# The first attention round of batch 0: transposes on TensorE, v in one piece, division after the product

## The chip, the cores and the metric

The kernel runs on one core of one Trainium2 chip. Its engines are named as in the profile: PE is TensorE, DVE is VectorE, ACT is ScalarE, POOL is GpSimd, SP is SyncE, which here only issues DMAs. The metric is the device time of one execution in microseconds (us). The time before is the median of three runs.

## The reference

Attention with pooled queries feeds a bilinear network. There are 4 batches of 8 heads, 1152 tokens and 64 columns a head; the network has 512 inputs and 1536 hidden columns.

```python
q_pool = q.reshape(B, H, S // 2, 2, D).mean(axis=3)
scores = (1 / sqrt(D)) * q_pool @ k.T                 # 576 x 1152 per head
attn = exp(scores - scores.max(-1)); attn = attn / (attn.sum(-1) + 1e-9)
x = (attn @ v), heads put side by side                # 2304 x 512
out = ((x @ w_a) * (x @ w_b)) @ w_out                 # 2304 x 512
```

All inputs and the output are fp32. q and k are drawn with a spread of about 0.55, the weights of the network come as 64-bit words (their float64 form), which the kernel turns into two parts each.

## The kernel before

**Blocks, passes, rounds.** Two heads make a pair, four pairs a batch. A block is 128 pooled queries (or 64 of both heads) of one head against its 1152 keys. Per block: `qk` puts the scores into PSUM (`sps`, two places of 1152 columns), `sm_max` (DVE, L692) copies them to `s` with their row maximum, `sm_exp` (ACT, L699) takes the exponential in place with its row sum, `sm_sum` and `sm_rec` (DVE) make the reciprocal of the sum, `sm_hi` (ACT, L712) writes the probabilities in fp16 to `p`, `sm_lo` (DVE, L716) the rest that fp16 lost, and one DMA transpose (SP, L722) brings both parts, keys in the partitions, to `pt`. After the two blocks of a row pair, `pv` (L752) multiplies them with v, which `v_hi` (ACT, L515) and `v_lo` (DVE, L518) have split into two fp16 parts as well: three products for each of 9 chunks of keys and both heads, 54 matmuls into `xps`. `x_copy`, `x_hi`, `x_lo` and `x_scale` bring the result to the input of the network, again in two parts.

Batch 0 takes two rounds: the first handles rows 0 to 255 of all four pairs ("even", passes 0 to 3, 16 blocks), the second the other rows. So tile 0 of the network (256 rows) can begin as soon as the first round is through. The scores of batch 0 and 1 are fp32 products.

**Weights.** For each of 12 groups f of 128 hidden columns there are three tiles m of 128x512: w_a, w_b and w_out. Each is loaded, and `w_abs` (ACT), `w_max` (DVE, L551, m < 2), `w_tail` (ACT), `w_sign` (POOL, L562) and `w_join` (DVE, L569) make one fp32 tile of the 64-bit words. `w_mag` (DVE, L577), `w_sum` (PE), `w_scale` and `w_inv` (DVE) make a common scale for m < 2; `w_hi` (ACT) and `w_lo` (DVE, L611; POOL, L616, for m = 2) split it.

**The network (MoE).** A tile t of 256 rows takes for each f 24 matmuls (`moe_mm`, L830), an eviction on ACT (`moe_a`, L837), one on DVE (`moe_g`, L842), then a split and `moe_o` (L856).

**Order.** Every step is declared with its engine, a planner's cost, and the names it reads and writes; the order on each engine is written out by hand in `ORDERS`, one list of step numbers per engine. At run time each engine takes its queue strictly in order.

```python
add("ACT", 1.15, i - 3.5, sm_hi, (i,), r=[s, t + "r"], w=[p + "h"])
add("DVE", 1.37 if ps_.split else 1.4, i - 3, sm_lo, (i,), r=[s, p + "h", t + "r"], w=[p + "l"], port=True)
add("SP", 2.97, i, transpose, (i,), r=[p + "h", p + "l"], w=[f"pt{slot}"], gen=0.42, block=1.02)
```

## Time and profile before

| what | value |
|---|---|
| median of 3 runs (lowest, highest) | 851.35 us (850.94, 855.6) |
| the profiled execution: its own time, its span | 852.03 us, 849.8 us |
| busy: PE, DVE, ACT, POOL | 771.8, 644.9, 580.9, 255.1 us |
| mean granted TensorE clock | 0.944 of full speed |
| DMA transposes (SP) | 144 |

The span runs from the first to the last instruction; the profiled execution's own time is 2.2 us longer. Busy time is the union of an engine's instructions; the mean of a group is that of one instruction and includes what overlaps the next.

### The profile page before, as it was taken

To read this page: it belongs to the slowest core of one execution; us is meant where nothing else is said; L and a number is where in the kernel's file an instruction comes from. 1 tells how busy PE (TensorE), PEld (TensorE's weight loads), DVE (VectorE), ACT (ScalarE), POOL (GpSimd) and SP (SyncE) were. 2 spreads that over 40 slices of the span, in tenths; PEclk is the share of its full clock that TensorE was granted. 3 is DMA by queue.
4 is the path that set the end of the run, shared out by engine and by line. 5 is a ranking of instruction groups with operands and counts; after the bars stand their busy time and mean duration, and the time that the engine had idled before them with its cause. 6 is when DMAs were issued, how large, how long until landed. Compare 5 with 4: busy or idle time off the path is not lost.

```text
span 849.8 us, 21268 instructions
## 1 busy us (share of the span) xinstructions
PE 771.8 (91%) x8832; PEld 591.2 (70%) x8832; DVE 644.9 (76%) x1240; ACT 580.9 (68%) x929; POOL 255.1 (30%) x230
## 2 busy tenths in 40 slices
...
GB/s 286 233 246 263 225 222 231 270 180 228 204 208 196 192 217 188 196 191 207 161 215 195 189 193 171 168 200 142 182 159 111 116 93 57 57 27 1 25 1 25
DMA packets 353664, 141.76 MB, mean 167 GB/s; under 512 B 338208, under 2 KB 340256, under 8 KB 353568
## 3 DMA queue, kind: packets, MB, share of 16 engines
...
q14 instruction: 27, 0.22, 0.1%
...
## 4 chain that ended last, share of the span: by engine, by line
PE 53%; DVE 2%; DMA 1%; issue 1%; ACT 0%
PE ab L830 24%; PE ab L856 14%; PE sps L660 8%; PE xps L752 7%; DMA pt<-p 1%; DVE p L716 1%; DVE s L692 1%; DVE g L842 0%; ACT g L837 0%; PE xps L485 0%; DVE vs L518 0%; DVE vmx L481 0%; DVE o L862 0%; PE xps L418 0%; DVE st L709 0%
## 5 line engine op out<-in xcount | busy, mean ns | idle before, releaser
L830 PEld LDWEIGHTS <-wab 128*128 128x128 f16 x2592 | 252.4, 98 | 35.2 <-issue 2.3
L830 PE MATMUL ab<-xt,wab 128*128 128x256 f16 x2304 | 262.3, 274 | 3.2 <-DVE g L842 3.2
L716 DVE SCALAR_TENSOR_TENSOR p<-s,st,p 128x1152 f16<-128x1152 f32 x144 | 206.7, 1439 | 20.1 <-ACT p L712 19.4
L712 ACT ACTIVATE p<-s,st 128x1152 f16<-128x1152 f32 x144 | 178.4, 1248 | 44.8 <-DVE st L709 13.5
L699 ACT ACTIVATE s<-s,st 128x1152 f32<-128x1152 f32 x144 | 179.6, 1248 | 34.6 <-DVE s L692 34.4
L850 POOL TENSOR_TENSOR gl<-g,gh 128x256 fp32r<-128x256 f32 x108 | 94.0, 877 | 328.9 <-ACT gh L847 295.0
L657 PE MATMUL sps<-k,q 64*128 64x512 f32 (+3 forms) x448 | 117.5, 620 | 56.5 <-DVE s L692 36.6
L856 PE MATMUL ab<-wo,gh 128*128 128x512 f32 x432 | 140.0, 405 | 1.7 <-DVE g L842 1.7
L657 PEld LDWEIGHTS sps<-k,q 64*128 64x128 f32 (+1 forms) x448 | 54.0, 210 | 118.8 <-issue 62.9
L752 PE MATMUL xps<-pt,vs 128*64 128x128 f16 (+1 forms) x4320 | 127.4, 219 | 6.6 <-DMA pt<-p 3.8
L752 PEld LDWEIGHTS <-vs 128*64 128x64 f16 x4320 | 117.8, 113 | 19.3 <-issue 16.0
L837 ACT ACTIVATE g<-ab,cc 128x256 f32<-128x256 f32 (+1 forms) x144 | 55.6, 416 | 97.4 <-PE ab L830 97.2
L692 DVE TENSOR_SCALAR_CACHE_REDUCE s<-sps,ksc 128x1152 f32<-128x1152 f32 x72 | 101.0, 1411 | 12.0 <-PE sps L660 11.2
L842 DVE SCALAR_TENSOR_TENSOR g<-ab,cc,g 128x256 f32<-128x256 f32 (+1 forms) x144 | 56.0, 412 | 70.4 <-ACT g L837 70.3
L692 DVE TENSOR_SCALAR_CACHE_REDUCE s<-sps 128x1152 f32<-128x1152 f32 x72 | 96.8, 1349 | 7.7 <-PE sps L657 7.1
L856 PEld LDWEIGHTS ab<-wo,gh 128*128 128x128 f32 x432 | 77.8, 188 | 20.1 <-ACT g L837 1.5
L856 PE MATMUL ab<-wo,gl 128*128 128x512 f32 x216 | 85.5, 396 | 0.0
L847 ACT ACTIVATE gh<-g 128x256 fp32r<-128x256 f32 x108 | 43.4, 411 | 48.5 <-PE ab L856 47.7
L660 PE MATMUL sps<-k,q 64*128 64x512 f16 (+3 forms) x624 | 65.4, 341 | 0.0
L660 PEld LDWEIGHTS <-q 64*128 64x128 f16 (+1 forms) x720 | 36.6, 97 | 39.9 <-issue 7.4
L562 POOL TENSOR_SCALAR xt<-xt 128x512 f16<-128x512 f32 x22 | 53.9, 2449 | 22.0 <-ACT xt L558 17.0
L856 PEld LDWEIGHTS ab<-wo,gl 128*128 128x128 f32 x216 | 40.6, 188 | 10.1 <-POOL gl L850 0.4
...
## 6 DMA issues: line engine op xcount, KB each, us to landing
...
pt<-p SPq DMA_TRANSPOSE x144, 5.5
```

Source lines behind the costliest of these rows:

```text
L657: nc.tensor.matmul(out, q, k, start=True, stop=True)
L660: nc.tensor.matmul(out, q[:, hq], k[:, hk], start=(hq, hk) == (0, 0), stop=(hq, hk) == (1, 0))
L692: nc.vector.tensor_scalar(out=s_t[sbuf(i)], in0=sps[:, at:at + S], scalar1=-1.0 / 16.0 if u is None else ksc[:, u, 4:5], scalar2=None, op0 ...
L699: nc.scalar.activation(out=s, in_=s, func=AF.Exp, scale=-1.0, bias=t[:, 0:1], accum_out=t[:, 1:2])
L712: nc.scalar.activation(out=p_t[pbuf(i)][:, 0], in_=s_t[sbuf(i)], func=AF.Copy, scale=st_t[i % NST][:, 3:4])
L716: nc.vector.scalar_tensor_tensor(out=p[:, 1], in0=s, scalar=st_t[i % NST][:, 3:4], in1=p[:, 0], op0=ALU.mult, op1=ALU.subtract)
L752: nc.tensor.matmul(xps[half(e), at:at + w], vs[:, c, e, hv], pt[:, hp, c, c0:c0 + w], start=(c == 0 and n == 0), stop=(c == NCH - 1 and n ...
L830: nc.tensor.matmul(dst if t < 8 else dst.rearrange("p (b n) -> p b n", b=B), wab[:, f, 1 - m, a, c], moe_x(t, b, c), start=(n == 0), stop= ...
L837: nc.scalar.activation(out=g_t[:, f, c], in_=ab[j][:, 1, c], func=AF.Copy, scale=cc[:, b, f, 0:1])
L842: nc.vector.scalar_tensor_tensor(out=g, in0=ab[j][:, 0, c], scalar=cc[:, b, f, 1:2], in1=g, op0=ALU.mult, op1=ALU.mult)
L850: nc.gpsimd.tensor_tensor(out=gl_t[j], in0=g_t[:, f], in1=gh_t[j].bitcast(F32), op=ALU.subtract)
L856: nc.tensor.matmul(acc[u], g[:, us], wo[:, f, a], start=(first and n == 0), stop=(last and n == 2))
```

## The change

In the four passes of the first round (`ps_.pe`, `N_PE = 4`), the probabilities are neither divided, split nor sent through a DMA. PE transposes the fp32 exponentials themselves against an identity matrix that POOL makes once (`unity`, in the MoE's g tile): 9 chunks of 128 columns per block, in groups of four or two into the two MoE accumulators (`acc`, that is `ab`), and ACT and DVE in turn (`EVICT`) copy each group to an fp32 view of `pt` (`tr_pe`, `tr_out`). `pv_f` multiplies with unsplit fp32 v, which is loaded alternately to the buffer of the split v and to `vraw`: 18 matmuls per row pair in place of 54. The division comes last: `r_diag` (ACT) writes the reciprocals onto a diagonal, `r_wide` (PE) spreads them over partitions beside the result in `xps`, `r_mul` (DVE) multiplies. v is still scaled by its pair's maximum, now in `x_copy`.

Of the weight steps, the magnitude is taken of the joined tile, by ACT for odd f (an absolute value with a sum) and by DVE for even f; the shift (`w_mag` before) is gone; and `w_lo` of m = 2 goes from POOL to DVE for even f. All five lists in `ORDERS` are new, and their numbers count the new steps, so only the first line of one is shown.

```diff
--- before.py
+++ after.py
@@ -27,6 +27,7 @@
 P_SCALE = 2.0 ** 14
 
 REMN = 64
+N_PE, EVICT = 4, "ADADA"
 N_WHOLE, TWO_ROUNDS = 2, (0,)
 
 XE, XR, XO = 0, 256, 320
...
@@ -54,155 +55,159 @@
 
 ORDERS = (
     (
-        13, 6, 21, 30, 38, 140, 148, 29, 157, 48, 165, 50, 67, 267, 94, 275, 121, 156, 284, 175, 292, 177, 394, 194,
...
+        12, 18, 7, 24, 26, 38, 28, 30, 32, 44, 34, 35, 54, 56, 151, 58, 52, 60, 62, 157, 64, 65, 163, 82, 177, 167,
...
@@ -386,6 +390,13 @@
     kz = [z_t[2][:, 128 * j:128 * j + 128] for j in range(2)]
     kzf = [x.bitcast(F16).rearrange("p (a n) -> p a n", a=2) for x in kz]
 
+    ident, diag = g_t[:, 0, 0:128], [g_t[:, 1 + e, 0:128] for e in range(2)]
+    ptf = pt.rearrange("p a c n -> p (a c n)").bitcast(F32).rearrange("p (a c n) -> p a c n", a=2, c=NCH)
+    vf = [vs.rearrange("p c e h d -> p (c e h d)").bitcast(F32).rearrange("p (c n) -> p c n", c=NCH), vraw]
+
+    def vbuf(p):
+        return (["vsh", "vsl"], ["vraw"])[p % 2] if p < N_PE else ["vraw"]
+
     pl = Plan()
     add = pl.add
...
@@ -520,9 +531,11 @@
         )
 
     def prep_vmax(p, new, key):
-        add("SP", 2.05, key - 3, load_v, (p,), w=["vraw"], lag=LOAD_LAG)
+        j = p % 2 if new and p < N_PE else 1
+        names = ["vraw"] if j else ["vsh", "vsl"]
+        add("SP", 2.05, key - 3, load_v, (p, j), w=names, lag=LOAD_LAG)
         if new:
-            add("DVE", 1.26, key, v_max, (p,), r=["vraw"], w=[f"vmx{p}"])
+            add("DVE", 1.26, key, v_max, (p, j), r=names, w=[f"vmx{p}"])
             add("PE", 0.22, key - 2, v_sum, (p,), r=[f"vmx{p}", "ones"], w=["xps"])
...
@@ -546,11 +559,17 @@
             out=z_t[zi(n)], in_=raw_t[ri(n)][:, :, 1].bitcast(F32), func=AF.Abs, scale=2.0 ** -112
         )
 
-    def w_max(f, m, n):
-        z = z_t[zi(n)]
-        nc.vector.tensor_scalar(
-            out=z, in0=z, scalar1=2.0 ** -126, scalar2=None, op0=ALU.max, op1=ALU.max, accum_out=wmx[:, f, m:m + 1]
-        )
+    def on_act(f):
+        return f % 2 == 1
+
+    def w_mag(f, m, n):
+        if on_act(f):
+            nc.scalar.activation(out=w_dst(f, m, 0), in_=w_src(m, n), func=AF.Abs, accum_out=wmx[:, f, m:m + 1])
+        else:
+            z = z_t[zi(n)]
+            nc.vector.tensor_reduce(
+                out=wmx[:, f, m:m + 1], in_=z, axis=AX.X, op=ALU.max, apply_absolute_value=True
+            )
 
...
@@ -612,6 +626,10 @@
                 out=w_dst(f, m, 1), in0=w_src(m, n), scalar=wsc[:, 0, f, m:m + 1], in1=w_dst(f, m, 0),
                 op0=ALU.mult, op1=ALU.subtract,
             )
+        elif f % 2 == 0:
+            nc.vector.tensor_tensor(
+                out=w_dst(f, m, 1), in0=w_src(m, n), in1=w_dst(f, m, 0).bitcast(F32), op=ALU.subtract
+            )
         else:
             nc.gpsimd.tensor_tensor(
...
             add("ACT", 0.555, key, w_tail, (n,), w=[rw + "l"], r=[rw])
             add("POOL", 2.5, key, w_sign, (n,), w=[rw + "l"], r=[rw], port=False)
             add("DVE", 0.68, key, w_join, (n,), r=[rw, rw + "l"], w=[z], port=True)
+            if m < 2:
+                last = [f"z{NZ + m}"] if f == NF - 1 else []
+                last += ["raw2"] if f == NF - 2 else []
+                if on_act(f):
+                    add("ACT", 0.66, key, w_mag, (f, m, n), r=[z], w=[f"wmx{f}{m}", f"w{f}{m}h"] + last)
+                else:
+                    add("DVE", 0.6, key, w_mag, (f, m, n), r=[z], w=[f"wmx{f}{m}"])
             if m == 1:
-                add("DVE", 0.07, key, w_mag, (f,), r=[f"wmx{f}0", f"wmx{f}1"], w=[f"wal{f}"])
-                add("PE", 0.2, key - 5, w_sum, (f,), r=[f"wal{f}", "ones"], w=["xps"])
...
+            elif f % 2 == 0:
+                add("DVE", 0.7, key, w_lo, (f, m, n), r=[z, f"w{f}{m}h"], w=[f"w{f}{m}l"], port=True)
             else:
                 add("POOL", 1.3, key, w_lo, (f, m, n), r=[z, f"w{f}{m}h"], w=[f"w{f}{m}l"])
 
@@ -724,6 +748,60 @@
             in_=p_t[pbuf(i)].rearrange("p a n -> p (a n)"),
         )
 
+    def unity():
+        nc.gpsimd.memset(ident, 0.0)
+        nc.gpsimd.affine_select(
+            out=ident, in_=ident, compare_op=ALU.not_equal, fill=1.0, base=0, pattern=[[-1, 128]], channel_multiplier=1
+        )
+
+    def tr_pe(chunks, j):
+        for n, (i, c) in enumerate(chunks):
+            nc.tensor.transpose(acc[j][:, 128 * n:128 * n + 128], s_t[sbuf(i)][:, 128 * c:128 * c + 128], ident)
+
+    def tr_out(chunks, j, on):
+        i, c = chunks[0]
+        m = 64 * (blocks[i].slot - blocks[i].head)
+        src = acc[j][:, 0:128 * len(chunks)].rearrange("p (c n) -> p c n", n=128)
+        dst = ptf[:, blocks[i].head, c:c + len(chunks), m:m + 128] if chunks[1][0] == i else ptf[:, :, c, m:m + 128]
+        if on == "A":
+            nc.scalar.activation(out=dst, in_=src, func=AF.Copy)
+        else:
+            nc.vector.tensor_copy(out=dst, in_=src)
+
+    def r_diag(i, e):
+        nc.scalar.activation(out=diag[e], in_=ident, func=AF.Copy, scale=st_t[i % NST][:, 3:4])
+
+    def r_wide():
+        for e in range(2):
+            nc.tensor.matmul(xps[half(e), 256:384], one.broadcast_to([128, 64]), diag[e], start=True, stop=True)
+
+    def r_mul(j, x0):
+        x = x32[j][:, x0:x0 + 128]
+        nc.vector.scalar_tensor_tensor(
+            out=x, in0=x, scalar=1.0 / P_SCALE, in1=xps[:, 256:384], op0=ALU.mult, op1=ALU.mult
+        )
+
+    def moved(ps_, i0, u):
+        parts = [[(i, c + d) for d in range(4)] for i in (i0, i0 + 1) for c in (0, 4)] + [[(i0, 8), (i0 + 1, 8)]]
+        out = []
+        for n, chunks in enumerate(parts):
+            j, w, on = (n + u) % 2, len(chunks), EVICT[n]
+            of = sorted(set(i for i, _ in chunks))
+            name = f"pt{blocks[i0].slot}x{n}"
+            out.append(name)
+            add("PE", 0.05 + 0.17 * w, i0 - 6, tr_pe, (chunks, j), r=[f"s{sbuf(i)}" for i in of] + ["g0"], w=[f"acc{j}"])
+            add("ACT" if on == "A" else "DVE", 0.07 + 0.11 * w if on == "A" else 0.07 + 0.14 * w, i0 - 3.5, tr_out, (chunks, j, on),
+                r=[f"acc{j}"], w=[name])
+        return out
+
+    def pv_f(p, at, m):
+        for c in range(NCH):
+            for e in range(2):
+                nc.tensor.matmul(
+                    xps[half(e), at:at + 128], vf[p % 2][:, c, 64 * e:64 * e + 64], ptf[:, e, c, m:m + 128],
+                    start=(c == 0), stop=(c == NCH - 1),
+                )
+
...
@@ -741,6 +819,10 @@
         add("ACT", 1.245, i - 3, sm_exp, (i,), r=[t + "m"], w=[s, t + "s"])
         add("DVE", 0.065, i - 5, sm_sum, (i,), r=[t + "s"], w=[t + "t"])
         add("DVE", 0.075, i - 5, sm_rec, (i,), r=[t + "t"], w=[t + "r"])
+        if ps_.pe:
+            e = blocks[i].head
+            add("ACT", 0.19, i - 3, r_diag, (i, e), r=[t + "r", "g0"], w=[f"g{1 + e}"])
+            return
         add("ACT", 1.15, i - 3.5, sm_hi, (i,), r=[s, t + "r"], w=[p + "h"])
         add("DVE", 1.37 if ps_.split else 1.4, i - 3, sm_lo, (i,), r=[s, p + "h", t + "r"], w=[p + "l"], port=True)
         add("SP", 2.97, i, transpose, (i,), r=[p + "h", p + "l"], w=[f"pt{slot}"], gen=0.42, block=1.02)
...
-    def x_copy(j, at, x0, w):
-        nc.scalar.activation(out=x32[j][:, x0:x0 + w], in_=xps[:, at:at + w], func=AF.Copy, scale=1.0 / P_SCALE)
+    def x_copy(j, at, x0, w, p):
+        scale = 1.0 / P_SCALE if p is None else vsc[:, p, 0:1]
+        nc.scalar.activation(out=x32[j][:, x0:x0 + w], in_=xps[:, at:at + w], func=AF.Copy, scale=scale)
 
     def unit(slots, at, w, key):
...
     def leave(ps_, at, x0, w, key):
         j = ps_.jx
-        add("ACT", 0.072 + 0.192 * w / 256, key - 4, x_copy, (j, at, x0, w), r=["xps"],
-            w=[f"x32{j}{c}" for c in range(x0 // 64, (x0 + w) // 64)])
+        add("ACT", 0.072 + 0.192 * w / 256, key - 4, x_copy, (j, at, x0, w, ps_.p if ps_.pe else None),
+            r=["xps"] + [f"vsc{ps_.p}"] * ps_.pe, w=[f"x32{j}{c}" for c in range(x0 // 64, (x0 + w) // 64)])
+        if ps_.pe:
+            add("DVE", 0.22, key - 4, r_mul, (j, x0), r=["xps"], w=[f"x32{j}{c}" for c in range(x0 // 64, (x0 + w) // 64)])
 
...
@@ -924,6 +1009,7 @@
             self.p, self.again, self.parts = p, again, parts
             self.ends = ()
             self.whole = b > 0
+            self.pe = n < N_PE
             self.split = b >= N_WHOLE
             self.u = n % 2
             self.jq, self.jx = 1 if self.split else n % 2, 0
@@ -976,17 +1062,18 @@
...
     def attend(m):
         ps_ = passes[m]
         b = ps_.p // NP
-        if not ps_.again:
+        if not ps_.pe and (not ps_.again or passes[m - 1].pe):
             prep_v(ps_.p, ps_.base - 1)
         split_qk(ps_, ps_.base - 8)
...
@@ -1000,7 +1087,14 @@
                 i += 1
             if r == 1 and nxt and not nxt.again:
                 prep_vmax(nxt.p, nxt.parts[0] == "even", ps_.end - 4)
-            unit(slots, at, w, i - 1)
+            if ps_.pe:
+                parts = moved(ps_, i - 2, r)
+                add("PE", 2.2, i - 10, pv_f, (ps_.p, at, 64 * slots[0]), r=[f"pt{t}" for t in slots] + parts + vbuf(ps_.p),
+                    w=["xps"], mode=2)
+                add("PE", 0.3, i - 10, r_wide, (), r=["g1", "g2", "ones"], w=["xps"], mode=2)
+                leaving = [(at, XE + at, 128)]
+            else:
+                unit(slots, at, w, i - 1)
             for span in leaving:
                 leave(ps_, *span, i - 1)
             if splits:
```

Three places show how the queues change. First PE, from the first row of the program after the opening scores. The rows of before (`sps` is the scores' PSUM, `xps` that of the product with v; the last two go on in the same way for the 54 matmuls of a row pair, and for those of the next):

```order
L657 MATMUL sps<-k_69,q_73 128x512 x4
L657 MATMUL sps<-k_69,q_73 128x128
L485 MATMUL xps<-vmx,one 128x2
L657 MATMUL sps<-k_69,q_73 128x128
L657 MATMUL sps<-k_69,q_73 128x512 x4
L657 MATMUL sps<-k_69,q_73 128x128 x2
L657 MATMUL sps<-k_68,q_74 128x512 x4
L657 MATMUL sps<-k_68,q_74 128x128 x2
L752 LDWEIGHTS vs
L752 MATMUL xps<-pt,vs 64x128
```

and of the changed kernel, from the first small sum on (`ab_100` and `ab_101` are the two accumulators, `s_75` and `s_76` the exponentials of the two heads, `g` the identity or the diagonal):

```order
L496 MATMUL xps<-vmx,one 128x2
L759 MATMUL ab_100<-g,s_75 128x128 x4
L759 MATMUL ab_101<-g,s_75 128x128 x4
L681 MATMUL sps<-k_69,q_73 128x512 x4
L681 MATMUL sps<-k_69,q_73 128x128
L759 MATMUL ab_100<-g,s_76 128x128 x4
L759 MATMUL ab_101<-g,s_76 128x128 x4
L759 MATMUL ab_100<-g,s_75 128x128
L759 MATMUL ab_100<-g,s_76 128x128
L681 MATMUL sps<-k_69,q_73 128x128
L800 MATMUL xps<-pt,vs 64x128 x18
L776 MATMUL xps<-g,one 64x128 x2
```

The next scores (L681) moved in between the transposes, and the product with v and the wide reciprocal (L800, L776) stand ahead of the third pair's scores.

Second ACT, from its first exponential on, before (`p` are the fp16 probabilities, `o`, `z`, `wab`, `xt` and `g` hold weights here):

```order
L699 ACTIVATE s_75,st<-s_75,st 128x1152
L515 ACTIVATE vs<-vraw,vsc 128x18x64
L712 ACTIVATE p_81<-s_75,st 128x1152
L699 ACTIVATE s_76,st<-s_76,st 128x1152
L558 ACTIVATE g<-g 128x512
L712 ACTIVATE p_82<-s_76,st 128x1152
L545 ACTIVATE z_91<-wab 128x512
L558 ACTIVATE wab<-wab 128x512
L545 ACTIVATE wab<-g 128x512
L699 ACTIVATE s_77,st<-s_77,st 128x1152
L699 ACTIVATE s_75,st<-s_75,st 128x1152
```

and in the changed kernel:

```order
L723 ACTIVATE s_75,st<-s_75,st 128x1152
L558 ACTIVATE z_91<-wab 128x512
L577 ACTIVATE g<-g 128x512
L723 ACTIVATE s_76,st<-s_76,st 128x1152
L767 ACTIVATE pt<-ab_100 128x4x128
L577 ACTIVATE xt_64<-xt_64 128x512
L558 ACTIVATE wab<-g 128x512
L772 ACTIVATE g<-g,st 128x128
L558 ACTIVATE o_90<-xt_64 128x512
L767 ACTIVATE pt<-ab_100 128x4x128
L621 ACTIVATE wo<-z_91 128x512
L767 ACTIVATE pt<-ab_100 128x2x128
```

The scaling to fp16 and v's split are gone; evictions (L767) and diagonals (L772) stand there, with more weight steps between two exponentials.

Third SP, whose queue holds all loads, near its start, before (`p` goes to `pt` by a DMA transpose):

```order
L539 DMA xt_64<-in_w_ab_dram 128x1024
L539 DMA wab<-in_w_out_dram 128x1024
L403 DMA qraw<-in_q_dram 128x2x256
L397 DMA vraw<-in_v_dram 128x1152
L722 DMA_TRANSPOSE pt<-p_81 128x18x128
L539 DMA xt_64<-in_w_out_dram 128x1024
L722 DMA_TRANSPOSE pt<-p_82 128x18x128
L539 DMA wab<-in_w_ab_dram 128x1024
L403 DMA qraw<-in_q_dram 128x2x256
L539 DMA g<-in_w_ab_dram 128x1024
L722 DMA_TRANSPOSE pt<-p_83 128x18x128
L722 DMA_TRANSPOSE pt<-p_81 128x18x128
```

and in the changed kernel:

```order
L414 DMA qraw<-in_q_dram 128x2x256
L552 DMA xt_64<-in_w_ab_dram 128x1024
L411 DMA k_68<-in_k_dram 128x1152
L552 DMA xt_64<-in_w_ab_dram 128x1024
L408 DMA vraw<-in_v_dram 128x1152
L552 DMA g<-in_w_ab_dram 128x1024
L552 DMA wab<-in_w_ab_dram 128x1024
L411 DMA k_69<-in_k_dram 128x1152
L414 DMA qraw<-in_q_dram 128x2x256
L552 DMA xt_64<-in_w_out_dram 128x1024 x2
L408 DMA vs<-in_v_dram 128x1152
L414 DMA qraw<-in_q_dram 128x2x256
```

The transposes of the first round are out of it, and the loads that stood behind them moved up; the first DMA transpose is now the 42nd entry of the queue, before it was the 13th.

## Rows read from the trace of the kernel before

**Rows 1.** The page, part 1: busy time, share of the span, instructions.
```profile
PE 771.8 (91%) x8832; PEld 591.2 (70%) x8832; DVE 644.9 (76%) x1240; ACT 580.9 (68%) x929; POOL 255.1 (30%) x230
```

**Rows 2.** Stretch, length, busy PE, PEld, DVE, ACT, POOL; granted clock, DMA share, GB/s.
```profile
10.00:151.40 141.40, 83.42 (x660) 51.68 (x657) 133.37 (x274) 117.09 (x173) 95.95 (x50) 0.67 0.99 242
10.00:153.50 143.50, 85.43 (x674) 53.19 (x671) 135.47 (x278) 118.35 (x176) 97.33 (x50) 0.68 0.98 241
147.10:250.00 102.90, 97.32 (x1249) 72.26 (x1248) 89.08 (x166) 80.19 (x123) 40.37 (x34) 0.98 1.09 218
250.00:800.00 550.00, 546.86 (x6629) 430.87 (x6629) 418.10 (x794) 373.84 (x613) 110.92 (x131) 1.00 0.80 150
50.00:60.00 10.00, 8.07 (x70) 5.35 (x69) 9.93 (x16) 9.87 (x19) 8.36 (x5) 0.56 0.98 264
150.00:160.00 10.00, 9.37 (x77) 6.92 (x74) 9.51 (x20) 8.46 (x15) 5.70 (x4) 1.00 0.93 319
```

**Rows 3.** Who waited for whom, 10 to 147 us: total, times, longest.
```profile
PE sps L657 <- DVE s L692: 34.6, 17, 3.7
```

**Rows 4.** DVE, 0 to 153 us, groups: busy us, mean ns, idle before them.
```profile
L716 DVE SCALAR_TENSOR_TENSOR p<-s,st,p 128x1152 f16<-128x1152 f32 x23 | 33.1, 1444 | 0.8 <-ACT p L712 0.7
...
L551 DVE TENSOR_SCALAR_CACHE_REDUCE o<-o 128x512 f32<-128x512 f32 x10 | 6.8, 676 | 3.9 <-ACT o L545 3.9
...
L577 DVE TENSOR_SCALAR wal<-wmx 128x2 int32<-128x2 int32 x11 | 4.7, 428 | 0.1
```

**Rows 5.** ACT, 0 to 151.4 us, groups of the same kind.
```profile
L699 ACT ACTIVATE s<-s,st 128x1152 f32<-128x1152 f32 x24 | 29.9, 1246 | 7.2 <-DVE s L692 7.2
L712 ACT ACTIVATE p<-s,st 128x1152 f16<-128x1152 f32 x23 | 28.3, 1244 | 5.8 <-DVE st L709 4.4 <-issue 1.4
L558 ACT ACTIVATE xt<-xt 128x512 int32<-128x512 uint32 x18 | 11.8, 657 | 4.6 <-DMA xt<-in_w_ab_dram 4.6
...
L782 ACT ACTIVATE xt<-x 128x256 f16<-128x256 f32 x4 | 1.6, 403 | 0.0
L761 ACT ACTIVATE x<-xps 128x256 f32<-128x256 f32 x4 | 1.4, 361 | 0.0
```

**Rows 6.** Groups by form over the whole run: evictions from PSUM.
```profile
L842 DVE SCALAR_TENSOR_TENSOR g<-ab,cc,g 128x256 f32<-128x256 f32 x96 | 45.6, 478 | 48.4 <-ACT g L837 48.2
...
L862 DVE COPY o<-ab 128x512 f32<-128x512 f32 x9 | 6.2, 687 | 34.2 <-PE ab L856 34.2
...
L864 ACT ACTIVATE o<-ab 128x512 f32<-128x512 f32 x9 | 5.3, 589 | 5.6 <-PE ab L856 5.6
```

**Rows 7.** PE in order of time: start us, length us, line, idle before.
```profile
7.11 3.69 PE L657 MATMUL sps<-k,q 64*128 64x512 f32 x10 [7.11 <-DMA k<-in_k_dram]
...
99.67 2.20 PE L657 MATMUL sps<-k,q 64*128 64x512 f32 x10
107.27 0.79 PE L657 MATMUL sps<-k,q 64*128 64x128 f32 x2 [5.40 <-DVE st L703]
...
112.18 4.07 PE L657 MATMUL sps<-k,q 64*128 64x512 f32 x10 [3.60 <-DVE s L692]
118.91 0.49 PE L657 MATMUL sps<-k,q 64*128 64x128 f32 x2 [2.66 <-DVE s L692]
...
147.12 1.48 PE L830 MATMUL ab<-xt,wab 128*128 128x256 f16 x12
```

**Rows 8.** The padded score product (L657), weight loads, 210 to 260 us.
```profile
L657 PEld LDWEIGHTS sps<-z,q x12: 186/188/189, 214.8 to 258.9; 128*128 128x128 f32 x12
```

**Rows 9.** Who writes pt, 0 to 147 us: ns min/median/max.
```profile
L722 SPq DMA_TRANSPOSE pt<-p x21: 2689/3979/5616, 18.0 to 144.3; - x21
```

**Rows 10.** ACT in order of time around its first MoE eviction.
```profile
149.70 0.66 ACT L558 ACTIVATE xt<-xt 128x512 int32<-128x512 uint32 x1
150.27 0.70 ACT L607 ACTIVATE wab<-wab,wsc 128x512 f16<-128x512 f32 x1
151.41 0.47 ACT L837 ACTIVATE g<-ab,cc 128x256 f32<-128x256 f32 x1 [0.43 <-PE ab L830]
```

23 lines of the change are left out of this document (9 added, 14 removed), and 284 rows, old and new, of the table ORDERS.

## Prediction

> **What bounds the kernel now.** I read the page first: PE is busy 91% of the span [rows 1]. Where the other 9% lie shows in busy time by stretch, which I cut where tile 0 of the MoE begins (first matmul 147.12 us, [rows 7]; first ACT eviction 151.41, [rows 10]). From 250 to 800 us PE is busy 546.9 of 550, from 147 to 250 it is 97.3 of 102.9: from 147 on PE is the bound and only work taken from PE can shorten that part [rows 2]. Before it, from 10 to 151.4, PE is busy 59% at a mean granted clock of 0.67, ACT 117.1 of 141.4 (83%), and DVE, to its own first MoE step at 153.5, 135.5 of 143.5 (94.4%) [rows 2]. Who waits for whom says the same: PE's largest wait is for L692, DVE's row maximum, 34.6 us [rows 3]. So the span is "DVE's work until tile 0 can start" plus about 700 us of PE work. A microsecond saved ahead of 147 on the engine that sets that point is a microsecond of the total.
>
> **The change, engine by engine, up to tile 0.** The PE queue of after has 78 score products ahead of the first MoE matmul (before: 83), the same v work and all MoE work behind it. So I count what stands in each queue ahead of its first MoE instruction, before and after, and price the difference with mean durations.
>
> DVE loses 16 low halves of p (23 to 7; 1.444 each, 23.1 us), 4 low halves of v of the same shape (5.8), 22 weight maxima (0.676, 14.9), 11 shifts (0.428, 4.7) and one row maximum with its small steps (1.6): 50.1 [rows 4]. It gains 16 evictions of four transposed chunks, priced as L862, a DVE copy of 128x512 out of PSUM (0.687, 11.0); 11 reductions of 512 columns and 6 further weight steps of that width (5 of them from POOL), 0.676 each by L551, 11.5; 8 multiplications by the reciprocal, at most L842's 0.478, 3.8 [rows 4, 6]. Net -23.8: 135.5 becomes 111.7.
>
> ACT loses 16 high halves of p and 4 of v (1.244 each, 24.9) and one exponential (1.246 + 0.19). It gains 16 evictions of four chunks (0.589 by L864), 8 of two chunks (0.361 by L761), 16 diagonals of 128 columns (0.30, taken below L782's 0.403 for 256), 10 magnitudes (0.657 by L558, plus an accumulator read of 0.19), 4 more copies out of xps (1.0 in all) and 3 weight steps that now stand ahead (2.0): 28.5 against 26.3 [rows 5, 6]. But successive ACT instructions overlap by 0.09 (one starts at 149.70, lasts 0.66, the next starts at 150.27, [rows 10]); 21 leave and 57 come (accumulator reads counted with their instruction), so 1.9 and 5.1 come off. Net about -1 to -2; I take -2: 115 us after 10 us. ACT's load stays, and **ACT becomes the longest queue**.
>
> PE gains most. Per row pair of the round, 18 transposes and 18 fp32 products with v replace 54 fp16 products. Prices at the two levels come from the score products: five of them 2.20 at the high clock and 4.07 at the low, the lone sixth 0.49 and 0.79 [rows 7]. 13 pairs of blocks: 35 us fast, 63 slow. A transpose is not in this trace. From below it costs one fp32 weight load of 128 columns, 0.188 [rows 8]; from above the lone product, 0.49. I take half a lone product, 0.24 (they run in fours, so the drain is shared): 144 make 35 fast (27 to 71), 58 slow. pv_f, 72 pairs that use both column halves as the score pairs use both row halves: 0.24 and 0.40 each, 18 and 29; if the halves didn't overlap, twice that. The wide reciprocal and the 14 small sums: 11 and 17. Sum 98 us fast, 167 slow, against 83 us busy now.
>
> SP loses 16 DMA transposes, each holding its queue for 3.98 us (median of 21 ahead of 147, [rows 9]), and the DMA engines, at a share of 0.99, lose their traffic [rows 2]. I cost this at nothing by itself, as it only lets loads come earlier. POOL loses 5 low halves, gains the identity matrix, and is busy 96 of 141 [rows 2]. The magnitude of a weight now stands behind POOL's sign step and DVE's join; the cover is the weight tiles of other f in flight. If it were gone, each of the 11 f would hold its w_hi back by about a join and a magnitude, 1.3 us, 15 in all.
>
> **The sum.** ACT needs 115 us after 10 us. At 100% its first MoE eviction comes at 125, at DVE's present share of 94.4% at 132, at ACT's own present 83% at 149. I take 90%, nearer to DVE's share, since ACT is now the queue that others wait for, but below it: DVE (112 in the same 128 us, 87%) and PE (77% if fast) are close behind, and in-order queues of like length lose more to each other than one long queue does. 115/0.90 = 128, so 138 instead of 151.4: 13.6 us earlier. Behind that point nothing is removed from PE; the five products that move behind it (2.2 us) I set against the 5.6 us that PE still idles from 147 to 250. Span 849.8 - 13.6 = 836.2; the profiled execution lies 2.2 above its span (852.03), so 838.4; the median shown, 851.35, is 0.7 below that: **838**.
>
> **The rivals.**
> *ACT and DVE use the room better* (low end). Shares of 94 to 100%: 832 down to 825. For it: loads come earlier, and DVE stops being everybody's wait. Against: an engine next to two nearly full ones.
>
> *A wait takes the place of the one removed.* The transposes go through two PSUM tiles (ab), so each group of four waits for the eviction two groups earlier, which stands in ACT's or DVE's queue behind weight steps; pv_f, the reciprocal and all small sums share one bank (xps), held until ACT's copy and DVE's multiplication are through. ACT's exponentials wait 7.2 us in 24 for DVE, 0.30 each [rows 5]; if the 40 new ACT instructions that wait for PE or DVE lose as much, that is 12 us: 849.8 - 13.6 + 12 gives about 850, no change.
>
> *PE becomes the bound, slower than before.* If PE stays at its low clock in round one, its 167 us, begun 7 us in as now [rows 7], end at 174, not 147: 27 us later, 878. It decides once less than 39% of this work runs at the high level (167 - 0.39 x 69 = 140, the time PE has today). For it: the granted clock is 0.67 now, and a stretch in which PE was busy 8.1 of 10 us had 0.56 [rows 2]. Against it: 9.4 of 10 had 1.00 [rows 2], and the products at 99.67, which came right behind other work, ran at the high level, while those at 107.27, after 5.4 us idle, ran low [rows 7]; more work in the same gaps means fewer such pauses. The Trainium skill (TensorE: Matmul & The Clock Gate, Part 4: PE-mode transpose) says that transposes don't count as busy for the clock, which stays low through them, and gives about 275 ns for one of bf16 in a kernel. By its price the fast sum would be 103 instead of 98 (an estimate from that page), and by its rule this rival is the likelier one; no row here shows a transpose on PE, so neither is borne out yet.
>
> **Chances.** 0.5% (4.3 us) is about what a measurement of this kernel can tell from no change. Forecast, 829 to 847: 0.58. Better than that: 0.10. The new wait, 847 to 855.6: 0.16. PE cold, up to 878: 0.16. The range that leaves no more than two in ten out reaches from ACT without a gap (825) into the first part of the cold case (857). Faster 0.68, same 0.16, slower 0.16; the forecast's own range is 829 to 847.
>
> **What would show it.** Right: the first MoE matmul near 134 and ACT's first MoE eviction near 138; ACT busy about 90% from 10 us to there, DVE below 90%; a granted clock above 0.67 in that stretch; transposes of 0.19 to 0.25; PE still above 99% from 250 to 800. Wrong: transposes at twice that with the clock at its low level; long waits of PE before L759 or L800 for evictions; ACT evictions that wait for PE; w_hi waiting for its scale; or a later part in which PE, now started earlier, waits for DMA transposes or DVE that it did not wait for before.

## The result, and the profile of the changed kernel

The changed kernel takes 841.27 us (median of four runs, 840.6 to 843.49), the kernel before 853.48 beside it (four runs, 850.94 to 855.6): a ratio of 0.986, 95% interval 0.982 to 0.990. It is faster by 1.4%. Forecast were 838 and a range of 825 to 857. The profiled execution took 841.28 us, with a span of 839.5. The same kernel run again as a control (experiment 5) gave 840.71 against 851.51, a ratio of 0.988 (0.986 to 0.990), so of the 13.4 us that were forecast 12.2 came in the first comparison and 10.8 in the second.

The page's first part answers to [rows 1]: PE has 11 us more work and a span that is 10.3 us shorter, DVE 24 us less, ACT as much as before.

```profile
PE 782.8 (93%) x8864; PEld 605.4 (72%) x8864; DVE 621.3 (74%) x1203; ACT 578.9 (69%) x978; POOL 248.5 (30%) x226
```

Busy time by stretch answers to [rows 2], with the same columns: stretch, length, busy PE, PEld, DVE, ACT, POOL, then granted clock, DMA share, GB/s. The first two rows end where ACT and DVE begin their first MoE step.

```profile
10.00:138.80 128.80, 95.93 (x696) 65.76 (x696) 111.69 (x242) 115.18 (x219) 90.42 (x47) 0.87 0.65 199
10.00:139.30 129.30, 96.43 (x698) 65.95 (x697) 112.17 (x243) 115.68 (x220) 90.92 (x47) 0.87 0.64 199
131.20:250.00 118.80, 116.36 (x1394) 86.84 (x1394) 103.23 (x185) 95.12 (x150) 40.59 (x34) 1.00 1.04 209
250.00:800.00 550.00, 539.56 (x6598) 427.82 (x6597) 407.23 (x778) 364.24 (x598) 111.47 (x129) 1.00 0.80 146
...
131.20:839.50 708.30, 690.15 (x8217) 543.24 (x8216) 515.02 (x971) 468.55 (x769) 160.88 (x175) 1.00 0.80 149
```

Read the ACT column of the first row and the DVE column of the second: 115.2 and 112.2 us, where the forecast had 115 and 111.7. ACT fills 89.4% of its stretch (taken: 90%), DVE 87%. The clock is 0.87 where it was 0.67, the DMA share 0.65 where it was 0.99. The fourth row is where the forecast fails: PE now idles 10.4 of these 550 us, before 3.1 [rows 2].

PE in order of time answers to [rows 7] (start, length, line, how many, idle time before). Between these rows lie products of scores and v, which aren't shown.

```profile
13.16 1.97 PE L759 MATMUL ab<-g,s 128*128 128x128 f32 x8
18.84 1.10 PE L759 MATMUL ab<-g,s 128*128 128x128 f32 x8
...
55.67 0.47 PE L759 MATMUL ab<-g,s 128*128 128x128 f32 x2 [1.45 <-ACT pt L767]
56.80 3.42 PE L800 MATMUL xps<-pt,vraw 128*64 128x128 f32 x36
...
80.37 2.19 PE L800 MATMUL xps<-pt,vs 128*64 128x128 f32 x36
...
109.95 4.11 PE L800 MATMUL xps<-pt,vraw 128*64 128x128 f32 x36
...
131.24 1.16 PE L915 MATMUL ab<-xt,wab 128*128 128x256 f16 x9
```

Eight transposes take 1.10 us in a stream, 0.137 each. The first eight took 1.97, as if at half the clock, although the granted clock is recorded as 1.00 there (13.2 to 15.1 us). The 36 records of a row pair are its 18 fp32 products with v, two passes each: 2.19 us at the high level (granted clock 1.00 from 80.4 to 82.4) and 4.11 at the low one (0.50 from 110 to 114), which is 0.24 and 0.46 for a pair of products where the forecast took 0.24 and 0.40. The last row is the first MoE matmul: 131.24, 15.9 us earlier than before [rows 7].

ACT's first MoE step (it answers to [rows 10]) comes at 138.79, 12.6 us earlier:

```profile
138.79 0.46 ACT L922 ACTIVATE g<-ab,cc 128x256 f32<-128x256 f32 x1
```

The new steps of ACT and DVE up to 139 us, grouped (busy us, mean ns, idle time before them and what ended it), answer to the prices taken from [rows 4 to 6]:

```profile
L767 ACT ACTIVATE pt<-ab 128x512 f32<-128x512 f32 x16 | 9.3, 580 | 3.5 <-PE ab L759 3.5
L772 ACT ACTIVATE g<-g,st 128x128 f32<-128x128 f32 x16 | 6.2, 390 | 0.0
L767 ACT ACTIVATE pt<-ab 128x256 f32<-128x256 f32 x8 | 2.9, 368 | 4.2 <-DMA pt<-p 4.2
```

```profile
L769 DVE COPY pt<-ab 128x512 f32<-128x512 f32 x16 | 10.9, 679 | 0.8 <-PE ab L759 0.8
L780 DVE SCALAR_TENSOR_TENSOR x<-x,xps 128x128 f32<-128x128 f32 x8 | 2.2, 280 | 4.2 <-ACT x L844 4.2
```

Who waited for whom on PE from 10 to 131 us (total, times, longest) answers to [rows 3]: the wait for row maxima has halved from 34.6, and the transposes' two tiles cost 5.5 us (4.1 and 1.4).

```profile
PE sps L681 <- DVE s L716: 16.5, 8, 5.7
PE ab L759 <- ACT pt L767: 4.1, 5, 1.4
...
PE ab L759 <- DVE pt L769: 1.4, 3, 0.8
```

**Where 5.6 us went.** Tile 0 begins 15.9 us earlier, the span shrinks by 10.3. PE is busy as long from its first MoE matmul to the end: 690.15 us in the last of the rows by stretch, 689.84 in the first row of the kernel before that follows. So the difference is idle time, 12.9 us before and 18.2 now. Two more rows of before and the same two of the changed kernel place it.

```profile
147.10:849.80 702.70, 689.84 (x8209) 541.88 (x8208) 513.67 (x973) 465.12 (x759) 160.06 (x177) 1.00 0.79 150
...
150.00:250.00 100.00, 94.42 (x1223) 69.64 (x1220) 86.21 (x160) 77.29 (x119) 37.55 (x33) 0.98 1.08 219
250.00:450.00 200.00, 198.30 (x2495) 149.40 (x2494) 183.18 (x333) 159.11 (x240) 42.09 (x47) 1.00 1.06 195
```

```profile
150.00:250.00 100.00, 98.44 (x1253) 73.16 (x1250) 86.01 (x152) 77.05 (x119) 27.06 (x27) 1.00 1.05 204
250.00:450.00 200.00, 191.78 (x2592) 145.19 (x2591) 186.90 (x341) 159.41 (x237) 40.28 (x44) 1.00 1.11 199
```

From 150 to 250 PE idles 1.6 us instead of 5.6; from 250 to 450, 8.2 instead of 1.7. In that stretch of the changed kernel PE waits for row maxima, which are not among its waits there before, and ACT waits 10.8 us for DMA transposes to give a buffer of p back (the kernel before: 5.1). First PE's waits, then ACT's:

```profile
PE sps L681 <- DVE s L716: 4.3, 4, 1.6
PE sps L684 <- DVE s L716: 1.3, 2, 1.0
```

```profile
ACT p L736 <- DMA pt<-p: 10.8, 7, 2.2
```

and the same of the kernel before, whose row maxima are L692:

```profile
PE sps L657 <- issue: 1.0, 1, 1.0
PE xps L752 <- DMA pt<-p: 0.7, 1, 0.7
```

```profile
ACT p L712 <- DMA pt<-p: 5.1, 4, 1.8
```

So a run can be read as three numbers: the first MoE matmul, 690 us of PE work, and the idle time behind. The experiments are told that way.

### The profile page after: what moved, and what is told of

Read it like the earlier page. It is cut to its first block, busy times and chain, and to the rows that moved or that the text cites. A ratio compares the mean times of both kernels' runs of the same rounds, so it can differ in the third digit from the quotient of the medians.

```text
span 839.5 us, 21299 instructions
## 1 busy us (share of the span) xinstructions
PE 782.8 (93%) x8864; PEld 605.4 (72%) x8864; DVE 621.3 (74%) x1203; ACT 578.9 (69%) x978; POOL 248.5 (30%) x226
## 4 chain that ended last, share of the span: by engine, by line
PE 44%; DVE 4%; DMA 2%; issue 1%; ACT 1%; ACTq 0%
PE ab L915 21%; PE ab L941 13%; PE sps L684 5%; PE xps L834 5%; DMA pt<-p 2%; DVE s L716 1%; DVE p L740 1%; DVE vs L529 0%; DVE vmx L492 0%; DVE k L448 0%; DVE g L927 0%; ACT g L922 0%; DVE o L947 0%; ACT s L723 0%; ACT p L736 0%
## 5 line engine op out<-in xcount | busy, mean ns | idle before, releaser
L740 DVE SCALAR_TENSOR_TENSOR p<-s,st,p 128x1152 f16<-128x1152 f32 x128 | 182.8, 1432 | 25.8 <-ACT p L736 25.3
L935 POOL TENSOR_TENSOR gl<-g,gh 128x256 fp32r<-128x256 f32 x108 | 98.1, 913 | 328.7 <-ACT gh L932 268.7
L736 ACT ACTIVATE p<-s,st 128x1152 f16<-128x1152 f32 x128 | 159.1, 1248 | 49.0 <-DMA pt<-p 16.7
L681 PE MATMUL sps<-k,q 64*128 64x512 f32 (+3 forms) x448 | 106.9, 570 | 31.5 <-DVE s L716 20.8
L681 PEld LDWEIGHTS sps<-k,q 64*128 64x128 f32 (+1 forms) x448 | 50.1, 193 | 86.3 <-issue 55.3
L834 PEld LDWEIGHTS <-vs 128*64 128x64 f16 x3888 | 100.2, 111 | 13.4 <-issue 11.5
L834 PE MATMUL xps<-pt,vs 128*64 128x128 f16 (+1 forms) x3888 | 108.6, 215 | 1.3 <-DMA pt<-p 1.1
L871 POOL TENSOR_TENSOR xt<-x,xt 128x256 f16<-128x256 f32 x32 | 23.1, 721 | 110.1 <-ACT xt L867 109.9
```

Source lines behind the costliest of these rows:

```text
L681: nc.tensor.matmul(out, q, k, start=True, stop=True)
L736: nc.scalar.activation(out=p_t[pbuf(i)][:, 0], in_=s_t[sbuf(i)], func=AF.Copy, scale=st_t[i % NST][:, 3:4])
L740: nc.vector.scalar_tensor_tensor(out=p[:, 1], in0=s, scalar=st_t[i % NST][:, 3:4], in1=p[:, 0], op0=ALU.mult, op1=ALU.subtract)
L834: nc.tensor.matmul(xps[half(e), at:at + w], vs[:, c, e, hv], pt[:, hp, c, c0:c0 + w], start=(c == 0 and n == 0), stop=(c == NCH - 1 and n ...
L935: nc.gpsimd.tensor_tensor(out=gl_t[j], in0=g_t[:, f], in1=gh_t[j].bitcast(F32), op=ALU.subtract)
```

## The experiments

Two things were open. What sets the start of tile 0: ACT alone, as the forecast had it, or the row of engines? And why does PE lose time from 250 to 450? Ratios are to the kernel before, on the same chip; first MoE matmuls, stretches and idle times are those of the profiled run.

**1. More work on ACT, on DVE, on PE.** On ACT, the scaled halves of ten weight blocks are written twice:

```
-        nc.scalar.activation(out=w_dst(f, m, 0), in_=w_src(m, n), func=AF.Copy, **scale)
+        for _ in range(2 if m < 2 and f < 5 else 1):
+            nc.scalar.activation(out=w_dst(f, m, 0), in_=w_src(m, n), func=AF.Copy, **scale)
```

> The changed kernel, with the scaled fp16 high half of each of the ten A and B blocks of weights 0 to 4 written twice on ACT (the same value again). That adds 10 evictions of 128x512 to ACT's queue ahead of its first MoE step; at 0.61 to 0.71 us each, the spacing and the duration of such steps in the changed kernel, 6 to 7 us. Theory (ACT is the longest queue: 115.2 us busy of the 128.8 from 10 us to its first MoE eviction at 138.8): that eviction comes 6 to 7 us later, near 145, the first MoE matmul near 137.5, and the time rises by 4 to 7 to 845 to 848. Rival (no queue is full, the PE waits for row maxima come from latencies along the chain, and ACT's 13.6 idle us take the work): the eviction moves by 2 us or less, time 841 to 843.

On DVE, their low halves are:

```
+            for _ in range(2 if f < 5 else 1):
                 nc.vector.scalar_tensor_tensor(
                     out=w_dst(f, m, 1), in0=w_src(m, n), scalar=wsc[:, 0, f, m:m + 1], in1=w_dst(f, m, 0),
```

> The changed kernel, with the low half of the same ten weight blocks written twice on DVE. It adds 10 steps of 128x512 to DVE; at 0.68 to 0.74 us each 7 us. Theory (queues; DVE has 112.2 us up to its first MoE step at 139.3, 3 less than ACT): DVE becomes the longest with 119; at the 94% that it reached in the kernel before this would be 10 + 127 = 137, so 0 to 5 us later than now at tile 0, and the time 841 to 846, less than for the same work on ACT. Rival (PE waits 16.5 us for row maxima on DVE, so DVE and not ACT is what the round waits for): tile 0 comes 7 us later or more, time 847 to 849, more than for the same work on ACT.

On PE, three of the five groups of transposes are done twice:

```
-        for n, (i, c) in enumerate(chunks):
+        for n, (i, c) in list(enumerate(chunks)) * (2 if chunks[0][1] != 4 else 1):
             nc.tensor.transpose(acc[j][:, 128 * n:128 * n + 128], s_t[sbuf(i)][:, 128 * c:128 * c + 128], ident)
```

> The changed kernel, with 10 of each 18 transposes of a row pair done twice on TensorE (three of the five groups, written again to the same place): 80 more transposes before tile 0, at 0.137 us each in a stream at the high clock 11 us, at 0.25 each in a low stretch 20 us. Theory (PE has room: it is busy 95.9 of 128.8 us up to 138.8, waits for its row maxima, and what it does more also keeps its clock up): tile 0 moves by less than 3 us, time 840 to 844. Rival (the transposes stand in the chain from exponential to eviction, or PE at its low clock is the limit): tile 0 comes 6 us later or more, time 847 to 858, and the granted clock of 10 to 138 falls below the 0.87 of now.

Measured: ACT 846.07 us, ratio 0.992 (0.991 to 0.994); DVE 845.65, ratio 0.992 (0.991 to 0.994); PE 836.6, ratio 0.983 (0.981 to 0.984). First MoE matmul at 136.0, 137.2 and 130.6. The stretch from 10 us to ACT's first MoE step with more on ACT, then with more on DVE:

```profile
10.00:143.60 133.60, 98.77 (x694) 68.62 (x695) 112.00 (x242) 122.42 (x229) 89.41 (x47) 0.82 0.62 192
```

```profile
10.00:144.80 134.80, 100.17 (x695) 67.40 (x695) 119.87 (x254) 117.41 (x221) 91.46 (x47) 0.84 0.62 192
```

Seven to eight more microseconds cost about the same on either engine: 5 us more than the control of experiment 5, or 4 by the ratios. For ACT this is what was expected (845 to 848). "Less on DVE than on ACT" fell, and so did "DVE and not ACT". What holds is plainer: the longest queue, whichever it is, fills 89 to 92% of the time to ACT's first MoE step (122.4 of 133.6, 119.9 of 134.8; the unaltered kernel 115.2 of 128.8). 80 more transposes on PE cost nothing at tile 0. That they made the run faster was not expected (840 to 844); the clock (experiment 5) and the idle time behind tile 0 (14.1 us, where the changed kernel has 18.2 and the control 17.0) are where it shows.

**2. Without the weight part, and the weight part alone.**

```
     def on_act(f):
-        return f % 2 == 1
+        return False
 ...
-        elif f % 2 == 0:
+        elif False:
             nc.vector.tensor_tensor(
```

The declaration of the same step and the lists of step numbers change with it.

> The changed kernel without its weight part: the magnitudes of odd weight blocks go back from ACT to DVE (all by the reduction), the low halves of even output weights back from DVE to POOL; the order of all other steps is that of the changed kernel. Up to tile 0 ACT loses 10 magnitudes (0.66 and a read of 0.19 each, in sequence some 7 us in all), DVE gains 10 reductions (0.68, 6.8) and loses 4 subtractions (0.69, 2.7): ACT 108, DVE 116. Theory (queues, and the weight part only shifts 7 us between two queues that are nearly even): DVE is the longest, at 90 to 94% full tile 0 begins 0 to 5 us earlier or later than now, time 838 to 846. Rival (the weight part is where the gain is, since DVE was the bound): most of it is lost, time 848 to 853.

Measured: 844.44, ratio 0.992 (0.989 to 0.994); first MoE matmul at 134.2. DVE's sum came out as written (116.0), ACT's 2 us above (110.2 for 108), and DVE is now the longest queue, at 88%:

```profile
10.00:141.70 131.70, 95.40 (x695) 65.36 (x695) 116.02 (x247) 110.19 (x198) 96.22 (x52) 0.84 0.63 195
```

The other half, with all five lists of ORDERS back in the order of before:

```
-N_PE, EVICT = 4, "ADADA"
+N_PE, EVICT = 0, "ADADA"
```

> The weight part of the change alone: the changed kernel's code with no head pair in the new form (N_PE = 0), so that batch 0 is as before, with the order of before and each weight step at its place there (a magnitude at the first place at which what it reads is there). Up to tile 0 DVE loses 22 maxima (14.9 us) and 11 shifts (4.7) and gains 11 reductions of 0.676 (7.4) and 4 subtractions of 0.69 (2.8): 9.4 less of 135.5; ACT gains 10 magnitudes of 0.66 with reads (7 to 8). Theory (DVE is the bound of that stretch, at 94%): the first MoE step of DVE comes 9.4 / 0.944 = 10 us earlier at most, 5 where ACT (125 of then 133 us) is in the way; time 844 to 849. Rival (the magnitude, which now stands behind POOL's sign step and DVE's join, delays the scales; and without an order of its own the saving is not used): tile 0 comes no earlier than before, time 851 to 858.

Measured: 865.6, ratio 1.017 (1.015 to 1.019), first MoE matmul at 156.5, 9.3 us later than before, although DVE has less to do. The rival holds, and more strongly than it was priced. PE's waits for the sums over a weight's magnitudes, from 10 to 147 us, first in the kernel before (for the shift and for the scales), then now:

```profile
PE xps L583 <- DVE wal L577: 3.0, 1, 3.0
PE xps L583 <- DVE wsc L591: 1.9, 1, 1.9
```

```profile
PE xps L594 <- ACT wab L564: 6.9, 2, 6.5
PE xps L594 <- DVE wmx L567: 6.6, 3, 3.2
```

So the attention part carries more than half of the gain: 0.992 without the weight part, 0.986 to 0.988 with it, intervals that touch. The weight part's magnitudes stand later in their chain, and in an order that isn't made for that they cost more than they save. The order of steps was not searched anew for either half, so what each could give with an order of its own stays open. Nor was a new order run on the kernel before. It alone can't explain the gain unless it moves DVE steps behind tile 0: DVE's 135.5 us of work, begun at 10 us and without a gap, would end at 145.5, and the changed kernel's first MoE step of DVE comes at 139.3.

**3. Less on DVE, or less for the DMA, from 225 to 450 us.** Six blocks without their low half (first edit), or without their transpose (second):

```
     def sm_lo(i):
         p, s = p_t[pbuf(i)], s_t[sbuf(i)]
+        if i in (40, 48, 56, 64, 72, 80):
+            return
```

> The changed kernel without the low half of p on DVE for six of the blocks of batches 1 and 2 (40, 48, 56, 64, 72 and 80; what the transposes then read there is an older block's low half, so the output is not the reference's). It takes 6 x 1.41 = 8.5 us from DVE between 225 and 450 us, where PE now idles 8.2 of 200 us, nearly all of it for row maxima on DVE. Theory 1 (DVE itself is too full there: 186.9 of 200 us): PE's idle time of 250 to 450 falls to 2 to 4 us and the time to 836 to 838. Theory 2 (the DMA transposes are too full there: 50 of them hold SP's queue for 175.5 of these 200 us, ACT and DVE wait behind them for a free buffer of p, and the row maxima stand behind in DVE's queue): DVE gains room but the buffers come free no sooner, PE still idles 6 us or more and the time is 840 to 842.

```
     def transpose(i):
+        if i in (40, 48, 56, 64, 72, 80):
+            return
```

> The changed kernel without the DMA transpose of the same six blocks (their products with v then read an older block's p, so the output is not the reference's); DVE and ACT do all that they did. It takes 6 x 3.5 = 21 us from SP's queue and the DMA engines between 225 and 450 us. Theory 2 (the DMA transposes are what is full): the waits of ACT for a free buffer of p (11.5 us in 250 to 450) fall to less than half, PE's idle time there falls from 8.2 to 2 to 4 us, time 835 to 837. Theory 1 (DVE is what is full): no effect beyond 1.5 us, 840 to 842.

Measured: 841.43, ratio 0.987 (0.984 to 0.989), and 838.41, ratio 0.984 (0.982 to 0.986). The stretch from 250 to 450 and ACT's wait for a buffer in it, first (two rows) with less on DVE, then with fewer transposes:

```profile
250.00:450.00 200.00, 193.32 (x2597) 145.67 (x2596) 181.29 (x334) 160.35 (x237) 40.40 (x44) 1.00 1.11 200
```

```profile
ACT p L736 <- DMA pt<-p: 11.1, 8, 2.3
```

```profile
250.00:450.00 200.00, 195.80 (x2622) 147.51 (x2619) 190.39 (x348) 161.80 (x240) 39.84 (x44) 1.00 1.02 189
```

```profile
ACT p L736 <- DMA pt<-p: 6.0, 7, 2.1
```

With 5.6 us less on DVE, PE still idles 6.7 us and ACT waits as long as ever: theory 1 falls. With fewer transposes PE idles 4.2 us and ACT's wait nearly halves: close to what theory 2 said (2 to 4 us, less than half), at a time 1.4 us above its range. Behind tile 0 (133.7 here, 134.4 with less on DVE) the idle time is 13.9 against 16.5.

That the transposes are the limit isn't shown by this. Two kernels with all of them and the same steps behind tile 0 (more on PE in experiment 1, products in experiment 5) idle only 4.3 us there too. The transposes hold SP's queue for 172 of the 200 us, before as well as after the change (the 175.5 in the expectation counts what reaches over the edges), and still for 164 with five fewer in the stretch. Nor is it the earlier tile 0: the kernels of experiment 1 with more on ACT and on DVE begin it 5 and 6 us later, and PE idles nearly as long from 250 to 450 (7.6 and 6.9 us):

```profile
250.00:450.00 200.00, 192.45 (x2582) 145.24 (x2580) 187.01 (x340) 159.95 (x236) 40.01 (x44) 1.00 1.10 198
```

```profile
250.00:450.00 200.00, 193.15 (x2594) 145.78 (x2593) 188.15 (x340) 161.36 (x238) 39.84 (x44) 1.00 1.11 199
```

**4. The order of before, behind tile 0's start and from 250 us on.** Only the lists of step numbers change (ORDERS), each time from one step on and on all engines alike:

```
 ORDERS, first steps of PE that differ (moe_mm of tile 0, column block 8; then of tile 1, block 4):
-        784, 597, 713, 792, 606, 601, 602, 802, 607, 611, 810, 731, 749, 827, 612, 766, 836, 616, 621, 617, 622, 844,
+        784, 597, 713, 792, 601, 602, 802, 810, 731, 749, 827, 766, 606, 836, 607, 611, 844, 783, 612, 857, 616, 617,
 ...
-        1027, 657, 660, 994, 1043, 885, 886, 1012, 889, 890, 1014, 1068, 893, 897, 894, 898, 1084, 901, 1026, 1042,
+        1027, 657, 660, 994, 1043, 885, 886, 1012, 889, 890, 1014, 1068, 893, 897, 894, 898, 1084, 1026, 1042, 1058,
```

> The changed kernel with the order of before on every engine for all steps behind the ninth weight column block of MoE tile 0 (near 155 us); the steps themselves and the order ahead of it are those of the changed kernel. Theory 3 (the loss of 5 us behind tile 0 is a property of the new order there): PE's idle time in 250 to 450 falls from 8.2 to the 1.7 of before, time 834 to 837. Theories 1 and 2 (DVE or the DMA transposes limit that stretch once tile 0 comes early, whatever the order): PE still idles 5 us or more there, time 840 to 846.

> The changed kernel with the order of before only from the fifth weight column block of MoE tile 1 on (near 250 us); up to there the new order. Theory 3 (the 8.2 us of idle PE in 250 to 450 belong to the new order of that stretch, the 1.6 us of 150 to 250 to the new order too): PE idles 2 us or less in 250 to 450 and 2 us in 150 to 250, the time is 5 to 6 us below the control, 834 to 837. Theory 2 (the DMA transposes limit 150 to 450 as a whole, and an order only chooses where PE waits for them): the waits come back at the seam or behind it, idle time of 150 to 450 stays at 6 to 10 us, time 839 to 843.

Measured: 840.75, ratio 0.987 (0.985 to 0.989), and 842.4, ratio 0.990 (0.987 to 0.992). Both stretches, with the order of before from 155 us on, then from 250 on:

```profile
150.00:250.00 100.00, 94.13 (x1231) 68.18 (x1229) 86.96 (x149) 76.96 (x119) 28.77 (x29) 0.98 1.05 208
250.00:450.00 200.00, 199.76 (x2631) 151.76 (x2630) 184.69 (x340) 160.38 (x240) 40.62 (x45) 1.00 1.04 193
```

```profile
150.00:250.00 100.00, 98.45 (x1257) 73.12 (x1255) 85.93 (x152) 77.20 (x121) 29.25 (x28) 1.00 1.05 206
250.00:450.00 200.00, 193.05 (x2600) 144.86 (x2599) 185.12 (x335) 159.77 (x236) 43.25 (x45) 1.00 1.05 194
```

The order of before takes the idle time out of 250 to 450 entirely (0.2 us), as theory 3 said, and pays for it with 5.9 us from 150 to 250; the time stays. Taking each order where it did best, the idle time is back at the seam and behind (1.6 and 7.0). Theory 3 is right on the place and wrong on the gain. Theories 1 and 2 had 5 us or more from 250 to 450 in the first kernel and fell there; theory 2's figures for the second came out (8.5 us of idle time from 150 to 450, 842.4).

**5. The control, and PE's clock.** The changed kernel unaltered; the kernel with the order of before from 250 us on and the 80 repeated transposes; and each transpose as an ordinary product with the identity:

```
-            nc.tensor.transpose(acc[j][:, 128 * n:128 * n + 128], s_t[sbuf(i)][:, 128 * c:128 * c + 128], ident)
+            nc.tensor.matmul(
+                acc[j][:, 128 * n:128 * n + 128], s_t[sbuf(i)][:, 128 * c:128 * c + 128], ident, start=True, stop=True
+            )
```

> The changed kernel again, unaltered, on the chip on which the next three run. Two profiles of the same first round differ so far: first MoE matmul at 131.2 us in the first profile of the changed kernel (granted clock 0.91 in 50 to 90), at 133.7 to 134.6 in the three kernels that differ from it only behind 150 us (0.83 there). Theory C (that is the clock's own spread, the same program having two outcomes): a median of 840 to 843 and a first MoE matmul at one of the two. Rival (the first profile was a stray and the kernel is slower): a median over 844 and tile 0 at 134 or later.

> The kernel before this one in the call, with the 80 repeated transposes of the run that added work to TensorE (its first round is the same program as there). Theory C (a TensorE that does more in the round keeps its clock: that run showed 1.00 and 0.96 in 10 to 50 and 50 to 90, where the other runs showed 0.88 to 0.96 and 0.82 to 0.91): again 0.95 or more in 50 to 90, first MoE matmul at 130 to 132 where the kernel without them shows 131 to 135, time 1 to 4 us below that kernel. Rival (that run's clock was chance): clock 0.83 to 0.91 in 50 to 90, tile 0 no earlier than without, time the same or up to 5 us longer.

> The changed kernel with each of the 144 transposes of the first round done as an ordinary fp32 matmul with the identity as the moving operand, to the same place. Two fp32 products of 128 columns take 0.49 us in the trace where eight transposes take 1.10, so one is taken at 0.24 instead of 0.137: PE does 15 us more up to tile 0, of 96 busy and 129 in all. The Trainium skill, page TensorE: Matmul & The Clock Gate, Part 4, says that transposes don't count as activity for the clock. By that rule the clock of 10 to 90 should rise clearly above that of the control (0.95 or more in 50 to 90 with tile 0 at 130 to 132) and above what repeated transposes gave. If a transpose counts as a matmul does (the run with 80 more transposes had the highest clock so far), the clock rises about as much as there, and tile 0 lies within 2 us of 131. If the 15 us stand in the way: tile 0 at 136 or later, time 845 to 850.

Measured: the control 840.71, ratio 0.988 (0.986 to 0.990), first MoE matmul at 131.9. The second 841.28, ratio 0.989 (0.986 to 0.991), at 130.2. The third 841.51, ratio 0.990 (0.988 to 0.992), at 133.2. The stretch from 50 to 90 us of the control, of the kernel of experiment 1 with more on PE, of its twin here, and with products:

```profile
50.00:90.00 40.00, 33.22 (x242) 21.87 (x240) 33.41 (x80) 36.84 (x75) 30.79 (x16) 0.83 0.52 181
```

```profile
50.00:90.00 40.00, 35.03 (x291) 25.45 (x292) 35.40 (x84) 38.97 (x80) 32.00 (x17) 0.96 0.59 196
```

```profile
50.00:90.00 40.00, 34.82 (x288) 25.20 (x288) 35.95 (x83) 38.98 (x80) 31.33 (x17) 0.96 0.58 192
```

```profile
50.00:90.00 40.00, 37.73 (x336) 29.98 (x334) 37.17 (x88) 39.93 (x81) 31.96 (x17) 1.00 0.59 200
```

With the repeated transposes the granted clock there is 0.96, twice; in six profiles of the same first round without them it is 0.91 once and 0.83 five times. Theory C holds for the clock. Tile 0 lies where it put it (130.2 and 130.6), but the control, at 0.83, is only 1.3 to 1.7 us later, so that the clock moved tile 0 isn't shown. For the time of the second kernel nothing is shown either: its median is 1.1 below its partner's, within the spread of both (839.2 to 845.8 and 838.3 to 845.6), and its profile is that of the slowest of its six runs. Done as products, the 144 transposes are 288 passes. Eight of them, 16 passes, take 2.05 us in a stream where eight transposes take 1.10:

```profile
23.86 2.05 PE L759 MATMUL ab<-g,s 128*128 128x128 f32 x16
```

So PE does 17 us more, at a clock of 1.00 from 50 to 90; tile 0 lies inside its usual spread (133.2), if a little outside the 2 us around 131 that were expected. PE has that much room. (The 0.49 us in the expectation is one product of two passes, not two products; the 0.24 taken from it was near the 0.256 measured all the same.)

## Why the prediction was right, step by step

**DVE was the bound of the first round, and taking work from it brings tile 0 forward: right in size.** DVE's queue fell to 112.2 us (111.7), the first MoE step of ACT came 12.6 us earlier (13.6). But less work on DVE isn't enough by itself: the weight part alone takes some from it, and tile 0 came 9.3 us later.

**ACT's load stays: right.** 115.2 (115), at 89.4% (90%). Single prices were off by more than the sum: the 16 diagonals take 0.390 instead of 0.30, and in DVE's sum the 8 multiplications 0.280 instead of 0.478.

**ACT becomes the longest queue: right as a sum, too strong as a cause.** Experiment 1 shows that DVE, 3 us shorter, costs as much when it is lengthened. The reading that held in six profiles, four of them above, is "the longest queue divided by 0.88 to 0.92", whichever engine it is on; in the others with the new first round, those with more on PE included, the share is 0.87 to 0.91. It belongs to this round: before the change it was 0.94, with the weight part alone 0.86.

**A microsecond ahead of 147 is one of the total: the step that failed, by 5.6 us.** The five products that move behind tile 0 were set against PE's idle time from 147 to 250, and nothing was put down for new waits. PE's busy time behind tile 0 in fact stayed the same (690.15 and 689.84), and its idle time grew by 5.3 us: 4.0 less in 150 to 250, 6.5 more in 250 to 450, 2.8 more elsewhere. The forecast named this place as the one that would prove it wrong. The first MoE matmul at 131.2 instead of 133.5 (147.1 less 13.6) made up for 2.3 of the 5.6, so the span came out 3.3 us and the time 3 us above the forecast. As that start varies by 3 us between profiles, how near the total came is in part luck. What the idle time comes from stays open. Without six transposes there is less of it, and ACT waits less; taking DVE work away changes little; an order moves it; a tile 0 that begins 5 us later leaves it. But two kernels that only do more on PE in the first round have as little of it with all their transposes (4.3 us in 250 to 450, more transposes and products alike). Why these hit fewer waits 150 us later, nothing here shows.

**PE: 98 us at the high clock, 167 at the low: near the first, by luck in part.** PE was busy 95.9 us up to 138.8, 7.1 of them behind tile 0's start, at a clock of 0.87. A transpose costs 0.137 in a stream, not 0.24. With 20 us for the transposes in place of 35 the fast sum would have been about 83 (an estimate from these rows); that PE was not at the high level throughout made up for it.

**SP's and the DMA's saving costed at nothing:** not tested, as no run puts that load back. The DMA share fell from 0.99 to 0.65 up to tile 0, and PE's largest wait there is still for row maxima.

**The rivals.** The new wait exists, but at 5.5 us on PE and 3.5 on ACT instead of 12. Another 4.2 on ACT, which the forecast didn't have, is one eviction that waits for a DMA transpose (in the grouped rows above). The PE that stays at its low clock didn't come. The Trainium skill (TensorE: Matmul & The Clock Gate, Part 4: PE-mode transpose) says that transposes don't count as busy for the clock; this case's rows speak against it, since with 80 more transposes the clock from 50 to 90 us was 0.96 instead of 0.83. They don't settle it: with products in place of transposes it was 1.00, as that rule would have it, but there PE was also busy for longer (37.7 of 40 us against 35). Its 275 ns, for bf16, is near the record of one fp32 transpose here (273 ns, median of 144), but in a stream one follows the other after 0.137 us. The skill's advice to use a transpose and not a standard matmul for it (Perfetto Trace Analysis, Transposes) agrees with the price, 0.137 against 0.256, but going against it cost no measurable time here.
